# Gated linear attention and top-1 experts on one core: fourth and fifth token chunk routed in one pass, three list steps and four weight casts moved to other engines

## The chip, the cores and the metric

One NeuronCore of a Trainium2 chip runs the whole kernel. Its engines are TensorE (PE in the rows; its weight loads are PEld), VectorE (DVE), ScalarE (ACT), GpSimd (POOL) and the queue engine SyncE (SP). Each engine works through its own instructions in a fixed order, and engines wait for each other by semaphores. The metric is the device time of one execution in microseconds (us); of several executions the median counts.

## What is computed

Two stages, one feeding the other. The first is a linear attention with a decaying state; the second sends every token to one of eight experts. An expert is the argmax of eight logits, except that a token whose local gate is at least 0.5 takes the expert of the token before it, so the choice runs through the sequence.

```python
for t in range(S):                                  # B=4, H=8, S=768, D=48
    state = alpha[:, :, t, :, None] * state + einsum('bhd,bhe->bhde', k[:, :, t], v[:, :, t])
    y[:, :, t] = einsum('bhd,bhde->bhe', q[:, :, t], state)
x = y as (B, S, 384)
for b in range(B):                                  # E=8 experts, F=1024
    for s in range(S):
        e = argmax(logits[b, s]) if s == 0 or local_gate[b, s] < 0.5 else prev_e
        p = softmax(logits[b, s])
        out[b, s] = p[e] * (relu(x[b, s] @ w1[e]) @ w2[e])
```

## The kernel before

The 3072 tokens are 24 **blocks** of 128 tokens: block i is batch i % 4, place i // 4. Four blocks, one of each batch, are a **chunk**; there are six chunks, counted from first to sixth.

**Attention.** The loop `for i in range(NB)` runs over the 24 blocks. `scan1(i + 2)` and `scan2(i + 2)` compute the running products of alpha two blocks ahead: DVE's scans `A` and `sf`, and after each a product on POOL into `ld`. `pm` (PE, PSUM tile `pz`), `mask` (DVE, `pq`), `kt` (`kp`, `kk`), `um` (`up`), `sums` (DVE, `st`), `qm` and `ym` (PE, `py`) make the block's output `XR`, which goes to DRAM (`xd`) and through PE (`xp`, `xx`) into the logits (`lg`, `lt`, `L`).

**Routing.** `route(g)` is a generator that runs for one group of chunks; `SPANS` sets the groups: first and second chunk together, then each of the four others alone. Between its yields the loop resumes it at marked places ("d" for DVE, "p" for PE, "g" for POOL), so that its work lies between that of the blocks. Its steps: the least negated logit `mx`, the comparisons `ge`, the two factors `kr` of the recurrence (DVE); their transposition `rp` (PE); copies `km` (ACT); the scan `em` along the sequence (DVE); back by `rb` (PE) to the one-hot experts `oh`; the counts `oi`, the probability (`ex`, `se`, `pn`, `facts`); the places `pw` (PE), `ps`, and `po`, `where` (DVE). Then each chunk's tokens are put into lists: `spots(a)` takes a place apart into high and low part (`zz`, `hi`, `lo` on POOL), makes the one-hot of the high part `hp` on DVE and its products with the facts on POOL, and the one-hot rows of the low part `lh` on ACT (`low`, five instructions); `lq` (PE) multiplies them, ACT copies the result, POOL adds it to `lists`.

**Early expert.** The first expert's tokens of the first twelve blocks (job `a`) are gathered (`xg_a`) and computed while attention still runs; its later tokens (job `b`) come from the last routing by `fast` (one-hot `hot`, PE `lp`, indices `ix_b`, gather `xg_b`, `tp_b`). Its weights come through three buffers `rw_a`; `Weights.split` makes a high part on ACT (`w1h`, `w2h`) and a remainder (`w1l`, `w2l`). The three pieces of w1 are cast on POOL in halves from the queue `pieces`, one half beside each scan; the four pieces of w2 are cast on DVE. A load into a buffer waits for the cast that frees it. PE's units `h_a` and `yp_a` of job `a` lie between the last blocks and the last routings.

**The rest.** When job `b` is done, seven more experts (`h_r`, `yp_r`) run one after the other.

The program order is kept on every engine (`pinned`, line 97 is the helper that records every operation); nothing is rescheduled.

```python
for w in (slice(0, F // 2), slice(F // 2, F)):
    halves.append(lambda w=w: cast(w, g_, 0.5))
...
for j in range(G):
    s_.activation(lh[:, j], rows[:, 0:128], AF.Abs, bias=lo[:, j:j + 1])
s_.activation(lh, lh, AF.Relu, bias=one[:, 0:1], scale=-1.0)
...
EW.split(SPLITS.index(i), pieces if i <= SPLITS[2] else None)
```

Of the kernel before, what the change touches and what calls it, by code (L numbers as in the profile page):

```python
# [36 lines left out]
G = B  # L37
SPANS = ((0, 2), (2, 3), (3, 4), (4, 5), (5, 6))
T1 = 12
# [33 lines left out]
def gla_moe(ctx, tc, akq, vw, vn, wg, w1, w2, cst, tok, out):  # L73
# [51 lines left out]
    fill = cp.tile([128, 3], F32, name="fill")  # L125
    where = cp.tile([128, NB], F32, name="where")
    facts = cp.tile([128, NB, 3], F32, name="facts")
# [22 lines left out]
    class Weights:  # L150
# [29 lines left out]
        def split(self, p, halves=None):  # L180
# [121 lines left out]
    with ac:  # L302
# [235 lines left out]
        def logits(c, lc):  # L538
            g, j, n = span[c * G]
            lt = pp.tile([128, G, 32], F32, tag="xp", name=f"lt_{c}")  # L540
            t_.transpose(lt.rearrange("p b e -> p (b e)"), lc, ident)
            if j == 0:
                grp[g] = ap.tile([128, n, E + 1], F32, tag=f"L{n}", bufs=1 + (n == G), name=f"L_{g}")
            s_.mul(grp[g][:, j:j + G], lt[:, :, 0:E + 1], -1.0)
            if j + G == n:
                steps.append([route(g), "d"])
            yield

        def route(g):
# [5 lines left out]
            def rt(shape, nm, dt=F32):  # L555
                return ap.tile(shape, dt, tag=f"{nm}{n}", bufs=1 + (n == G and nm in ("pl", "ix", "ps", "em")), name=f"{nm}_{g}")

            L = grp.pop(g)
            L8 = L[:, :, 0:8]
            kr = ap.tile([128, 2, G * max(y - x for x, y in SPANS), 8], F32, tag="kr", bufs=1, name=f"kr_{g}")[:, :, 0:n]  # L560
            ex = rt([128, n, 8], "ex")
# [21 lines left out]
            k0 = km[:, 0]  # L583
            if cb < NBB:
                s_.copy(km, rp)
            else:
                s_.copy(km[:, 1], rp[:, 1])
                k0 = rp[:, 0]
# [40 lines left out]
            xf = where[:, G * ca:G * cb]  # L629
            po = rt([128, n, 8], "po")  # L630
# [8 lines left out]
            while busy[0]:  # L639
                yield "p"  # L640
            high, low, parts = spots(ca)
            for a in range(ca, cb):
                yield "d"
                while not parts:
                    yield "d"
                high()
                yield "p"
                low()
                yield "h" if cb == NBB else "p"
                while len(parts) < 2:  # L650
                    yield "p"
                lq = pp.tile([128, 3 * E * 4], F32, tag="xp", name=f"lq_{a}")
                for j in range(G):
                    t_.matmul(lq, lhsT=lh[:, j], rhs=hp[:, j].rearrange("p c k -> p (c k)"), start=(j == 0), stop=(j == G - 1))
                la = lists.rearrange("p c k -> p (c k)")
                ln = hp[:, 0].rearrange("p c k -> p (c k)") if a else la
                s_.copy(ln, lq)
# [80 lines left out]
        def col(shape, nm, dt=F32):  # L738
            return ap.tile(shape, dt, bufs=1, name=nm)
# [121 lines left out]
        for i in range(NB):  # L861
# [71 lines left out]
        while any(r[1] != "h" for r in steps):  # L933
# [274 lines left out]
```

## Time and profile before

| what | value |
|---|---|
| median of 3 runs | 416.35 us (416.0 to 417.12) |
| the profiled execution itself | 415.97 us |
| its span in the trace | 414.0 us |
| PE busy | 386.2 us (93%) |
| DVE busy | 248.4 us (60%) |
| ACT busy | 182.1 us (44%) |
| POOL busy | 162.6 us (39%) |

The span is the traced stretch from the first to the last instruction; the time of the execution holds some 2 us more around it. The busy shares are means over stages that differ: attention, the last routings beside job `a`, job `b`, and the seven experts. A name in a row, as `po<-ps,oh`, is the tile written and the tiles read.

### The profile page before, as it was taken

The page shows a single profiled execution, that of the slowest core. Times are in us where ns is not written, and L with a number is a line of the kernel's source. Part 1 is how long each engine was busy: PE and PEld are TensorE (multiplying, and loading weights), DVE is VectorE, ACT ScalarE, POOL GpSimd, SP SyncE. Part 2 cuts the span into 40 slices and gives each one's busy share as a digit, 9 for nine tenths or more (in the row PEclk, how much of TensorE's full clock was granted, in tenths as well). Part 3 has the DMA queues.
Part 4 walks back from the last instruction along what each step waited for, and adds up shares of the span by engine and source line. Part 5 has one row for each costly group of instructions (what it writes and reads, how often), then busy time and mean ns, then how long its engine had stood idle before and what let it go on. Part 6 is the DMA issues. An engine that isn't in the chain of part 4 may idle for free.

```text
span 414.0 us, 11455 instructions
## 1 busy us (share of the span) xinstructions
PE 386.2 (93%) x4563; PEld 355.9 (86%) x4563; DVE 248.4 (60%) x569; ACT 182.1 (44%) x450; POOL 162.6 (39%) x232
## 2 busy tenths in 40 slices
PE   7899998989899979999999999999999999999990
PEld 7798877778787869998899999999899899999990
DVE  8879989999887443474572554454364364564310
ACT  2267766678746540362541451352252352453200
POOL 7448666666574010543511432341241241512010
PEclk9889999999999995899999999999999999999996
DMA  8959898887724000564463264175076075461010
GB/s 227 236 161 238 234 296 211 247 229 189 213 62 142 33 8 0 184 194 153 133 180 118 74 198 150 32 234 166 20 220 181 21 222 177 141 185 55 1 40 7
DMA packets 25849, 60.15 MB, mean 145 GB/s; under 512 B 4836, under 2 KB 11318, under 8 KB 25794
## 3 DMA queue, kind: packets, MB, share of 16 engines
q1 hardware_dynamic: 22066, 49.22, 42.2%
q0 software_dynamic: 3584, 10.04, 7.1%
q8 instruction: 36, 0.59, 0.6%
q14 instruction: 19, 0.16, 0.1%
q10 hardware_dynamic: 144, 0.14, 0.1%
HBM read 49.95 MB, written 10.04 MB: 145 GB/s over the span
## 4 chain that ended last, share of the span: by engine, by line
PE 59%; DVE 18%; issue 12%; DMA 4%; POOL 3%; ACT 2%; SPq 0%; DVEq 0%; POOLq 0%; ACTq 0%
PE yp_r L97 19%; PE h_r L97 18%; DVE sf L97 6%; DVE A L97 4%; PE pz L97 3%; DMA ld<-akq 3%; PE yp_a L97 3%; PE py L97 3%; PE yp_b L97 2%; PE h_b L97 2%; PE h_a L97 2%; PE tp_r L97 2%; DVE pq L97 2%; PE up L97 1%; POOL out L97 1%
## 5 line engine op out<-in xcount | busy, mean ns | idle before, releaser
L97 POOL DMA_INDIRECT out<-yo_r,ix_r x25 | 24.7, 987 | 125.2 <-DVE yo_r L97 98.6
L97 PE MATMUL yp_r<-w2h_r,hh_r 128*128 128x384 f32 (+4 forms) x200 | 68.9, 345 | 0.0
L97 PE MATMUL yp_r<-w2h_r,hl_r 128*128 128x384 f32 (+4 forms) x200 | 67.3, 337 | 0.0
L97 PE MATMUL yp_r<-w2l_r,hh_r 128*128 128x384 f32 (+4 forms) x200 | 67.2, 336 | 0.0
L97 PE MATMUL h_r<-xh_r,w1h_r 128*128 128x384 f32 (+5 forms) x168 | 59.9, 356 | 1.0 <-DVE yo_b L97 0.8
L97 PE MATMUL h_r<-xl_r,w1h_r 128*128 128x384 f32 (+5 forms) x168 | 59.6, 355 | 0.0
L97 PE MATMUL h_r<-xh_r,w1l_r 128*128 128x384 f32 (+5 forms) x168 | 59.6, 355 | 0.0
L97 ACT ACTIVATE hh_r<-h_r 128x384 fp32r<-128x384 f32 (+5 forms) x56 | 29.4, 525 | 68.4 <-PE h_r L97 68.2
L97 DVE SCALAR_TENSOR_TENSOR hl_r<-h_r,hh_r 128x384 fp32r<-128x384 f32 (+5 forms) x56 | 33.3, 597 | 33.9 <-ACT hh_r L97 33.6
L97 DVE TENSOR_TENSOR_SCAN sf<-ld,sf,zp 112x128 f32<-112x128 f32 x96 | 38.3, 462 | 0.9
L97 PEld LDWEIGHTS yp_r<-w2l_r,hh_r 128*128 128x128 f32 (+4 forms) x200 | 36.1, 181 | 1.1
L97 PEld LDWEIGHTS yp_r<-w2h_r,hl_r 128*128 128x128 f32 (+4 forms) x200 | 36.0, 180 | 1.2
L97 PEld LDWEIGHTS yp_r<-w2h_r,hh_r 128*128 128x128 f32 (+4 forms) x200 | 36.1, 180 | 1.1
L97 POOL DMA_INDIRECT xg_r<-xd,ix_r x25 | 27.6, 1104 | 19.9 <-PE h_r L97 8.5
L97 ACT CAST xh_r<-tp_r 128x384 fp32r<-128x384 f32 (+4 forms) x25 | 11.4, 455 | 54.2 <-PE tp_r L97 54.2
L97 POOL TENSOR_TENSOR ld<-ld,A 112x512 f32<-112x512 f32 x24 | 28.4, 1182 | 16.5 <-DVE A L97 11.7
L97 PEld LDWEIGHTS h_r<-xh_r,w1h_r 128*128 128x128 f32 x168 | 31.6, 188 | 3.6 <-issue 1.1
L97 POOL TENSOR_TENSOR ld<-ld,sf 112x512 f32<-112x512 f32 x24 | 28.4, 1184 | 14.5 <-DVE sf L97 14.5
L97 PEld LDWEIGHTS h_r<-xh_r,w1l_r 128*128 128x128 f32 x168 | 31.5, 188 | 2.0
L97 PEld LDWEIGHTS h_r<-xl_r,w1h_r 128*128 128x128 f32 x168 | 31.5, 188 | 1.8
L97 DVE TENSOR_SCALAR yo_r<-yp_r,pr 128x384 f32<-128x384 f32 (+4 forms) x25 | 15.4, 616 | 29.4 <-PE yp_r L97 29.4
L97 DVE TENSOR_TENSOR_SCAN A<-ld,zp 112x260 f32<-112x260 f32 x48 | 30.8, 683 | 2.5
(205 smaller groups left out, 795.1 us busy)
## 6 DMA issues: line engine op xcount, KB each, us to landing
rw_r<-w SPq DMA_DIRECT2D x21, 512.0 KB, 4.4
rw_r<-w SPq DMA_DIRECT2D x28, 384.0 KB, 3.6
ld<-akq SPq DMA_DIRECT2D x44, 192.0 KB, 4.4
vt<-vn SPq DMA_DIRECT2D x24, 192.0 KB, 3.5
xd<-XR SPq DMA_DIRECT2D x24, 192.0 KB, 4.1
ld<-akq SPq DMA_DIRECT2D x44, 97.7 KB, 4.5
rw_a<-w SPq DMA_DIRECT2D x3, 512.0 KB, 5.1
rw_a<-w SPq DMA_DIRECT2D x4, 384.0 KB, 4.2
```

The source lines that it names most:

```text
L97: r = f(*a, **k)
```

## The change

The third and fourth group of `SPANS` become one of two chunks, so that the fourth chunk is routed with the fifth, after attention's last block. In `route`, the subtraction `ex` moves ahead of the comparison and serves it (one comparison with zero and multiplication in one instruction), the two transpositions `rp` become one, and the reductions `pn` and `where` become one over `both`. After attention (`drained`), the lists are made by `at_once`: `zz`, `hi`, `lo`, `hp` and `lh` all on DVE, in buffers of their own. The four pieces of the early expert's w2 are cast by POOL, each in one instruction.

```diff
-SPANS = ((0, 2), (2, 3), (3, 4), (4, 5), (5, 6))
+SPANS = ((0, 2), (2, 3), (3, 5), (5, 6))
...
-                for w in (slice(0, F // 2), slice(F // 2, F)):
-                    halves.append(lambda w=w: cast(w, g_, 0.5))
+                for w in (slice(0, F // 2), slice(F // 2, F)) if n < 3 else (slice(None),):
+                    halves.append(lambda w=w: cast(w, g_, 0.5 if n < 3 else 1))
...
+            v_.tensor_tensor(ex, L8, mb, ALU.subtract)
             ge = rt([128, n, 8], "ge")
-            v_.tensor_tensor(ge, L8, mb, ALU.is_le)
-            v_.tensor_tensor(ge, ge, cc("desc").unsqueeze(1).broadcast_to([128, n, 8]), ALU.mult)
+            v_.scalar_tensor_tensor(ge, ex, 0.0, cc("desc").unsqueeze(1).broadcast_to([128, n, 8]), ALU.is_le, ALU.mult)
...
-            for j in range(2):
-                for c in range(m):
-                    t_.transpose(rp[:, j, c * 128:(c + 1) * 128],
-                                 kr[:, j, G * c:G * (c + 1)].rearrange("p b e -> p (b e)"), ident)
+            for c in range(m):
+                t_.transpose(rp[:, c * 128:(c + 1) * 128], kr[:, c].rearrange("p j b e -> p (j b e)"), ident)
...
-            v_.tensor_tensor(ex, L8, mb, ALU.subtract)
...
-            v_.tensor_tensor(ex, ex, ob, ALU.mult)
-            pn = rt([128, n], "pn")
-            v_.tensor_reduce(pn, ex, AX.X, ALU.add)
-            v_.tensor_tensor(facts[:, G * ca:G * cb, 0], pn, se, ALU.mult)
+            po = rt([128, 2, n, 8], "po")
+            v_.tensor_tensor(po[:, 0], ex, ob, ALU.mult)
...
-            v_.tensor_tensor(po, ps[:, :, 0:n].rearrange("p e b -> p b e"), ob, ALU.mult)
-            v_.tensor_reduce(xf, po, AX.X, ALU.add)
+            v_.tensor_tensor(po[:, 1], ps[:, :, 0:n].rearrange("p e b -> p b e"), ob, ALU.mult)
+            v_.tensor_reduce(both[:, :, G * ca:G * cb], po, AX.X, ALU.add)
+            v_.tensor_tensor(facts[:, G * ca:G * cb, 0], both[:, 0, G * ca:G * cb], se, ALU.mult)
...
             for a in range(ca, cb):
+                if drained[0]:
+                    if cb == NBB:
+                        yield "d"
+                    rr = at_once(a)
+                    yield "h" if cb == NBB else "p"
+                    if a == ca and m > 1:
+                        yield "p"
+                    product(a, *rr)()
+                    continue
...
+        def at_once(a):
+
+            lh = ap.tile([128, 2, HP, C], F32, tag="pq", bufs=2, name=f"lh_{a}").rearrange(
+                "p e h t -> p (e h t)").rearrange("p (j t) -> p j t", j=G)
+            hp = ap.tile([128, DM], F32, tag="XR", bufs=3, name=f"hp_{a}").rearrange("p (j c k) -> p j c k", j=G, c=3)
+            x = where[:, G * a:G * (a + 1)]
+            f = facts[:, G * a:G * (a + 1)]
+            z, hi, lo = (ap.tile([128, G], F32, tag=t, bufs=1, name=f"{t}_{a}") for t in ("zz", "hi", "lo"))
+            v_.tensor_scalar(z, x, 1.0 / 128, MAGIC, ALU.mult, ALU.add)
+            v_.tensor_scalar(hi, z, MAGIC + BASE / 128, 128.0, ALU.subtract, ALU.mult)
+            v_.tensor_tensor(hp[:, :, 0], hv.unsqueeze(1).broadcast_to([128, G, E * 4]),
+                             hi.unsqueeze(2).broadcast_to([128, G, E * 4]), ALU.is_equal)
+            for c in (2, 1, 0):
+                g_.tensor_tensor(hp[:, :, c], hp[:, :, 0], f[:, :, c:c + 1].broadcast_to([128, G, E * 4]), ALU.mult)
+            v_.tensor_tensor(lo, x, hi, ALU.subtract)
+            for j in range(G):
+                v_.tensor_scalar(lh[:, j], rows[:, 0:128], lo[:, j:j + 1], None, ALU.is_equal)
+            return lh, hp
...
-                EW.split(SPLITS.index(i), pieces if i <= SPLITS[2] else None)
+                EW.split(SPLITS.index(i), pieces)
...
         drained[0] = True
+        while pieces:
+            pieces.pop(0)()
...
-        EW.split(6)
+        EW.split(6, pieces)
+        while pieces:
+            pieces.pop(0)()
```

How the order moves, at three places. First DVE in the last iteration that scans, between the mask `pq` of block 21 and the end of the scans of block 23. Before:

```order
L97 TENSOR_TENSOR pq_2676<-pz,cs 128x512
L97 SCALAR_TENSOR_TENSOR oi_2678<-m_111,oh_109 128x40
L97 TENSOR_REDUCE se_2680<-ex_2426 128x4
L97 TENSOR_SCALAR se_2680<-se_2680 128x4
L97 RECIPROCAL se_2680<-se_2680 128x4
L97 TENSOR_TENSOR ex_2426<-ex_2426,oh_109 128x32
L97 TENSOR_REDUCE pn_2685<-ex_2426 128x4
L97 TENSOR_TENSOR facts<-pn_2685,se_2680 128x4
L97 TENSOR_TENSOR w2l_a_2647<-rw_a_1881,w2h_a_2646 128x768
L97 MEMSET ld_116 112x4
```

and in the change:

```order
L97 TENSOR_TENSOR pq_2645<-pz,cs 128x512
L97 MEMSET ld_116 112x4
L97 SCALAR_TENSOR_TENSOR A_2679<-ld_116,zp 112x260 x2
L97 RECIPROCAL sf_2685<-A_2679 112x4
L97 SCALAR_TENSOR_TENSOR sf_2685<-ld_116,sf_2685,zp 112x128 x4
L97 TENSOR_TENSOR st_2344<-up_2670,st_2344 112x192
```

The fourth chunk's seven instructions and a cast have left DVE here; nothing stands between mask and scan. Its other instructions have left the two iterations before and the one after in the same way.

Second DVE after the transposed gathers of job `a` (`xl_a`), at the routing that follows the mask of block 23. Before, the fifth chunk alone (32 elements a row):

```order
L97 TENSOR_TENSOR pq_2927<-pz,cs 128x512
L97 TENSOR_TENSOR hp<-hv,hi_2811 128x4x32
L97 TENSOR_REDUCE mx_2932<-L_2849 128x4
L97 TENSOR_TENSOR ge_2934<-L_2849,mx_2932 128x32
L97 TENSOR_TENSOR ge_2934<-ge_2934,cs 128x32
L97 TENSOR_REDUCE m_3_2937<-ge_2934 128x4
```

and in the change, fourth and fifth together (64 elements a row):

```order
L97 TENSOR_TENSOR pq_2870<-pz,cs 128x512
L97 TENSOR_REDUCE mx_2874<-L_2342 128x8
L97 TENSOR_TENSOR ex_2873<-L_2342,mx_2874 128x64
L97 SCALAR_TENSOR_TENSOR ge_2877<-ex_2873,cs 128x64
L97 TENSOR_REDUCE m_2_2879<-ge_2877 128x8
```

The chain has as many instructions as before, and the fourth chunk's `hp` no longer stands ahead of it.

Third POOL, from the last product of attention to the gathers of job `b`. Before:

```order
L97 TENSOR_TENSOR ld_116<-ld_116,sf_2733 112x512
L97 TENSOR_SCALAR zz_2810<-where 128x4
L97 TENSOR_SCALAR hi_2811<-zz_2810 128x4
L97 TENSOR_TENSOR lo_2812<-hi_2811,where 128x4
L97 TENSOR_TENSOR hp<-hp,facts 128x4x32 x3
L97 TENSOR_TENSOR lists<-hp,lists 128x96
```

and in the change:

```order
L97 TENSOR_TENSOR ld_116<-ld_116,sf_2685 112x512
L97 TENSOR_TENSOR w2l_a_2616<-rw_a_1877,w2h_a_2615 128x768
L97 TENSOR_TENSOR w2l_a_2728<-rw_a_2264,w2h_a_2727 128x768
L97 TENSOR_TENSOR w2l_a_2841<-rw_a_2618,w2h_a_2840 128x768
L97 TENSOR_TENSOR w2l_a_3030<-rw_a_2843,w2h_a_3029 128x768
L97 TENSOR_TENSOR hp_3089<-hp_3089,facts 128x4x32 x3
L97 TENSOR_TENSOR lists<-hp_3089,lists 128x96
```

POOL's small place arithmetic is gone, and four casts stand ahead of the fourth chunk's products.

## Rows read from the trace of the kernel before

**Rows 1.** Page, part 2: busy tenths and TensorE's clock in 40 slices.

```profile
DVE  8879989999887443474572554454364364564310
PEclk9889999999999995899999999999999999999996
```

**Rows 2.** Chain that ended last: start us, us, engine, tile written, instructions.

```profile
130.28 1.33 PE h_a L97 x9
...
145.33 0.86 PE pw L97 x6
...
174.83 8.31 PE h_b L97 x72
...
193.68 17.04 PE h_r L97 x72
```

**Rows 3.** Timeline, DVE: start us, us, operation, out<-in, count; routing in attention.

```profile
76.30 0.22 DVE L97 TENSOR_REDUCE pn<-ex 128x8 f32<-128x64 f32 x1
...
108.54 0.18 DVE L97 TENSOR_REDUCE mx<-L 128x4 f32<-128x32 f32 x1
...
110.12 0.06 DVE L97 MEMSET ld<- 112x4 f32 x1 [0.19 <-issue]
...
114.31 0.57 DVE L97 TENSOR_TENSOR_SCAN em<-km,em 32x128 f32<-32x128 f32 x1
...
114.92 0.06 DVE L97 MEMSET ld<- 112x4 f32 x1
...
120.74 0.23 DVE L97 TENSOR_TENSOR_SCAN oi<-m,oh 128x40 f32<-128x40 f32 x1
...
122.15 0.95 DVE L97 TENSOR_TENSOR w2l_a<-rw_a,w2h_a 128x768 fp32r<-128x768 f32 x1
123.05 0.06 DVE L97 MEMSET ld<- 112x4 f32 x1
```

**Rows 4.** Timeline, PE: `qm` of blocks 20 and 21; in brackets, idle before and releaser.

```profile
120.28 0.68 PE L97 MATMUL py<-st,ld 48*64 48x48 f32 x30 [0.60 <-DVE st L97]
...
126.59 0.68 PE L97 MATMUL py<-st,ld 48*64 48x48 f32 x30 [0.44 <-DVE st L97]
```

**Rows 5.** Timeline, PE: the last routings.

```profile
134.82 0.38 PE L97 MATMUL rp<-cs,kr 128*32 128x128 f32 x2 [0.30 <-DVE kr L97]
...
138.03 1.13 PE L97 MATMUL lq<-hp,lh 128*128 128x96 f32 x8
139.54 0.55 PE L97 MATMUL xp<-cs,XR 128*128 128x128 f32 x3 [0.39 <-ACT hp L97]
...
154.03 1.89 PE L97 MATMUL lq<-hp,lh 128*128 128x96 f32 x8 [1.89 <-DVE ex L97]
156.31 0.31 PE L97 MATMUL rb<-cs,em 32*128 32x32 f32 x1 [0.38 <-ACT hp L97]
```

**Rows 6.** Timelines of POOL, DVE and ACT: instructions side by side, and casts.

```profile
123.21 1.27 POOL L97 TENSOR_TENSOR w1l_a<-rw_a,w1h_a 128x512 fp32r<-128x512 f32 x1 [0.37 <-DVE ld L97]
...
126.37 1.19 POOL L97 TENSOR_TENSOR ld<-ld,sf 112x512 f32<-112x512 f32 x1 [0.60 <-DVE sf L97]
...
127.05 0.58 DVE L97 TENSOR_TENSOR po<-ps,oh 128x32 f32<-128x32 f32 x1
...
131.93 0.83 ACT L97 CAST w2h_a<-rw_a 128x768 fp32r<-128x768 f32 x1
...
132.91 0.28 DVE L97 TENSOR_TENSOR hp<-hv,hi 128x128 f32<-128x128 f32 x1
...
146.45 0.22 DVE L97 TENSOR_TENSOR po<-ps,oh 128x32 f32<-128x32 f32 x1 [0.69 <-ACT ps L97]
```

**Rows 7.** PE's first longer wait; then two stretches: PE busy (x), PEld, DVE, ACT, POOL, PEclk, DMA.

```profile
16.50 0.67 PE L97 MATMUL py<-st,ld 48*64 48x48 f32 x16 [1.26 <-DVE st L97]
...
17.70:24.20 6.50, 6.50 (x92) 5.87 (x91) 4.15 (x11) 2.03 (x8) 2.35 (x2) 0.50 0.68 154
154.20:167.60 13.40, 13.02 (x51) 12.71 (x51) 4.67 (x27) 0.72 (x4) 2.52 (x4) 0.50 0.05 13
```

More of the change, by code (lines that the diff above doesn't have):

```diff
@@ L125, in gla_moe @@
     fill = cp.tile([128, 3], F32, name="fill")
-    where = cp.tile([128, NB], F32, name="where")
+    both = cp.tile([128, 2, NB], F32, name="both")
+    where = both[:, 1]
     facts = cp.tile([128, NB, 3], F32, name="facts")
@@ L555, in rt @@
             def rt(shape, nm, dt=F32):
-                return ap.tile(shape, dt, tag=f"{nm}{n}", bufs=1 + (n == G and nm in ("pl", "ix", "ps", "em")), name=f"{nm}_{g}")
+                return ap.tile(shape, dt, tag=f"{nm}{n}", bufs=1, name=f"{nm}_{g}")
             L = grp.pop(g)
             L8 = L[:, :, 0:8]
-            kr = ap.tile([128, 2, G * max(y - x for x, y in SPANS), 8], F32, tag="kr", bufs=1, name=f"kr_{g}")[:, :, 0:n]
+            kr = ap.tile([128, max(y - x for x, y in SPANS), 2, G, 8], F32, tag="kr", bufs=1, name=f"kr_{g}")[:, 0:m]
             ex = rt([128, n, 8], "ex")
@@ L572, in route @@
             v_.tensor_tensor(ge, ge, m2.unsqueeze(2).broadcast_to([128, n, 8]), ALU.is_equal)
-            zb = L[:, :, 8:9].broadcast_to([128, n, 8])
-            v_.scalar_tensor_tensor(kr[:, 0], zb, -ZTHR, ge, ALU.is_gt, ALU.mult)
-            v_.tensor_single_scalar(kr[:, 1], zb, -ZTHR, ALU.is_le)
+            zb = L[:, :, 8:9].rearrange("p (c b) e -> p c b e", b=G).broadcast_to([128, m, G, 8])
+            v_.scalar_tensor_tensor(kr[:, :, 0], zb, -ZTHR, ge.rearrange("p (c b) e -> p c b e", b=G), ALU.is_gt, ALU.mult)
+            v_.tensor_single_scalar(kr[:, :, 1], zb, -ZTHR, ALU.is_le)
             yield "p"
-            rp = pp.tile([8 * G, 2, m * 128], F32, tag="xp", name=f"rp_{g}")
-            for j in range(2):
-                for c in range(m):
-                    t_.transpose(rp[:, j, c * 128:(c + 1) * 128],
-                                 kr[:, j, G * c:G * (c + 1)].rearrange("p b e -> p (b e)"), ident)
+            rp = pp.tile([16 * G, m * 128], F32, tag="xp", name=f"rp_{g}")
+            for c in range(m):
+                t_.transpose(rp[:, c * 128:(c + 1) * 128], kr[:, c].rearrange("p j b e -> p (j b e)"), ident)
             km = ap.tile([8 * G, 2, 128 * max(y - x for x, y in SPANS)], F32, tag="km", bufs=1, name=f"km_{g}")[:, :, 0:m * 128]
-            k0 = km[:, 0]
+            s_.copy(km[:, 1], rp[8 * G:])
+            k0 = rp[0:8 * G]
             if cb < NBB:
[L585 to L588, printed above, removed]
+                s_.copy(km[:, 0], k0)
+                k0 = km[:, 0]
             yield "d"
@@ L640, in route @@
                 yield "p"
-            high, low, parts = spots(ca)
+            if not drained[0]:
+                high, low, parts = spots(ca)
             for a in range(ca, cb):
+                if drained[0]:
[7 more added lines that the diff above has]
+                    continue
                 yield "d"
@@ L648, in route @@
                 low()
-                yield "h" if cb == NBB else "p"
+                yield "p"
                 while len(parts) < 2:
                     yield "p"
[L652 to L657, printed above, removed]
+                add = product(a, lh, hp)
                 busy[0] = False
@@ L661, in route @@
                 yield "g"
-                if a:
-                    g_.tensor_tensor(la, ln, la, ALU.add)
-                listed.append(a)
+                add()
             if cb * G == T1:
@@ L669, in route, with product, add @@
                 gathers.append(0)
+        def product(a, lh, hp):
+            lq = pp.tile([128, 3 * E * 4], F32, tag="xp", name=f"lq_{a}")
+            for j in range(G):
+                t_.matmul(lq, lhsT=lh[:, j], rhs=hp[:, j].rearrange("p c k -> p (c k)"), start=(j == 0), stop=(j == G - 1))
+            la = lists.rearrange("p c k -> p (c k)")
+            ln = hp[:, 0].rearrange("p c k -> p (c k)") if a else la
+            s_.copy(ln, lq)
+            def add():
+                if a:
+                    g_.tensor_tensor(la, ln, la, ALU.add)
+                listed.append(a)
+            return add
+        def at_once(a):
[12 more added lines that the diff above has]
+            v_.tensor_tensor(lo, x, hi, ALU.subtract)
+            for j in range(G):
+                v_.tensor_scalar(lh[:, j], rows[:, 0:128], lo[:, j:j + 1], None, ALU.is_equal)
+            return lh, hp
         def spots(a):
@@ L937, in gla_moe @@
             n += 1
-        both = col([128, 2, E], "both")
+        rest = col([128, 2, E], "rest")
         pick3 = big
         v_.tensor_tensor(pick3, hot8.rearrange("p r e -> p e r"), caps.unsqueeze(1).broadcast_to([128, E, E]), ALU.mult)
-        v_.tensor_reduce(both[:, 0], pick3, AX.X, ALU.add)
-        v_.tensor_tensor(both[:, 1], cF, both[:, 0], ALU.subtract)
+        v_.tensor_reduce(rest[:, 0], pick3, AX.X, ALU.add)
+        v_.tensor_tensor(rest[:, 1], cF, rest[:, 0], ALU.subtract)
         jobs = [jb]
@@ L965, in gla_moe @@
         ct = pp.tile([8, 2, 128], F32, tag="kp", name="ct")
-        t_.transpose(ct[:, 0], both[:, 0], ident)
-        t_.transpose(ct[:, 1], both[:, 1], ident)
+        t_.transpose(ct[:, 0], rest[:, 0], ident)
+        t_.transpose(ct[:, 1], rest[:, 1], ident)
         v_.tensor_copy(capp, ct[:, 0, 0:1])
```

3 lines of the change are left out of this document (1 added, 2 removed).

## The prediction, made before the changed kernel ran

> **What bounds the kernel now.** I read the busy tenths first, then the chain of waits, then the timelines engine by engine around what the change moves. Each of the 40 slices is 10.35 us long. DVE stands at 8 or 9 tenths up to the 13th slice, and the clock row shows one slice near half speed, the 16th [rows 1]. So attention, up to about 126 us, goes at DVE's pace, and an instruction that leaves DVE there can shorten it. The chain then changes over to PE: from the first `h_a` at 130.28 us it runs through PE's work, job b starts at 174.83 and the first of the seven experts at 193.68 [rows 2]. The edits end before `h_b`, and what follows is the same code with its own loads behind the same gather. A shift at `h_b` is therefore a shift of the end. I work out that shift; minus means earlier. The profiled execution took 415.97 us, 0.38 under the median of 416.35; sums stand against it, and 0.4 is added for forecasts.
>
> **Attention: fewer instructions on DVE.** The first two groups each lose two small instructions. A reduction of 64 elements takes 0.22 us, one of 32 takes 0.18 [rows 3], and the joint reduction is longer by that difference or two of them; I take -0.3 for a group, -0.6 for both, between 0 (if a wait swallows it) and -0.9.
>
> The fourth chunk leaves three iterations at DVE's pace: from `mx` to the next memset 110.12 - 108.54 = 1.58, from `em` 114.92 - 114.31 = 0.61, from `oi` 123.05 - 120.74 = 2.31 us, the last with a cast from 122.15 to 123.05 [rows 3]. The first two count in full. In the third, PE becomes the slower one. PE's `qm` waited for DVE's `st` at 120.28 and again at 126.59, the second time 0.44 us [rows 4]. Between the two lie 6.31 us; without that wait and without a `pw`, 0.86 [rows 2], PE needs 5.0, while DVE would need 6.31 - 2.31 = 4.0. So this iteration gives 6.31 - 5.0 = 1.3. Together -(0.6 + 1.58 + 0.61 + 1.3) = **-4.1** at `h_a`, between -5.1 (DVE alone) and -3.1 (one of ACT's or the loads' steps takes back 1 us). The transpositions and copies that are merged or split ride under DVE here and count nothing; should PE or ACT be last somewhere, that is the 1 us.
>
> Queues: POOL's gathers `xg_a` stand ahead of the casts and are not delayed. On SP, the load of the last early weight piece moves behind one store, since its buffer now comes free only after POOL's first cast. What covers that: its cast on ACT stands behind the last block's `ym`, two units of `h_a` later. Nothing on DVE or PE asks for a `w2l` before `yp_a`, after `rb`.
>
> **After attention: a wait that the casts bring.** At 126.37 POOL began a product of 1.19 us, to 127.56; DVE's `po` beside it took 0.58 us from 127.05, to 127.63, where the same instruction with POOL idle took 0.22 [rows 6]. So a DVE instruction that reads two tiles of SBUF is held until POOL's instruction ends. POOL casts half a piece, 512 columns, in 1.27 us [rows 6]; a w2 piece has 768, so 1.27 x 768/512 = 1.9. Before, DVE made these casts.
>
> The third cast waits for ACT's `w2h`, which in the rows ended at 131.93 + 0.83 = 132.76; both it and DVE's mask hang on the first `h_a`, so they keep their distance. POOL starts at about 132.86. DVE's chain for `kr` now starts where `hp` stood, 132.91 [rows 6]. Its pace is 1.58/7 = 0.23 per instruction at 32 elements [rows 3], 0.26 at 64. Its second instruction, the first with two inputs in SBUF, wants to start at 133.17, finds POOL busy and is held to 134.76. Six instructions of 0.26 later, 136.3, `rp` can go. PE is there at 134.82 - 0.30 = 134.52 [rows 5]: it waits 1.8 us instead of 0.30, **+1.5**. The bounds are -0.1 (no hold: the chain ends at 134.73) and +1.9 (held for a whole cast). I take +1.5, because `po` was held to the end of POOL's instruction and not merely slowed. If the two only slowed each other as much as that row shows, 0.58 - 0.22 = 0.36, the chain would end near 135.1 and the sum below would be 1.2 less.
>
> The Trainium skill's page "SBUF — State Buffer" (section "Who interferes with whom") has a rule that speaks against this change: a VectorE instruction with two SBUF inputs and a GpSimd instruction that reads SBUF share one read interface, and whichever starts first keeps it for its whole instruction. By that rule the hold is a whole cast's; the trace agrees as far as it goes, since `po` ended 0.07 us after POOL [rows 6], but it shows no hold as long as 1.9 us.
>
> **After attention: what goes and what comes.** The fourth chunk's `lq` leaves its place: 139.54 - 138.03, **-1.5** [rows 5]. It comes back beside the fifth's. Before, from the last `h_a` to `rb`: `lq` at 154.03 had waited 1.89 for ACT's `lh`, so that `h_a`, 1.33 long [rows 2], began at 150.8, and 5.5 us passed to 156.31 [rows 5]. Now two `lq` with their copies, 1.5 each, one `h_a` of 1.3, and a short wait for POOL's products, taken as 0.4 (estimate: the list's addition and three products beside one `h_a`), make 4.7: **-0.8**, between -1.9 (the old wait goes whole) and 0. `lh` and `hp` on DVE count nothing: before the first `lq` they lie under two `h_a`, 2.6 us; without that cover they would cost their length, some 2 us.
>
> **The clock.** PE had 1.2 GHz in two stretches: 17.7 to 24.2, soon after a wait of 1.26 us, and 154.2 to 167.6, after the wait of 1.89 [rows 5, 7]. In the second, `yp_a`, `pw` and `lp` ran. In the change the wait of 1.89 goes, but short `lq`, waits and small matmuls follow each other there, so I leave the clock in the last routing as it was: 0. The bounds: 0, and half of the 11.3 us from `rb` to 167.6, -5.7, if it stays at 2.4 GHz.
>
> **Sum:** -4.1 + 1.5 - 1.5 - 0.8 = -4.9; 415.97 - 4.9 = 411.1, on the median **411.4 us**.
>
> **Rivals.**
>
> No hold at `rp`: -4.9 - 1.6 = -6.5, 409.9. For it: 0.3 us of order decides who comes first. Against: the cast lasts longer than the whole chain.
>
> The clock stays at 2.4 GHz through the last routing: PE would gain up to 5.7 but then wait for DVE's indices and the gather of job b, which a faster PE doesn't shorten; between 0 and 5.7 I take -3.5: -8.4, 408.0. For it: the long wait is gone. Against: the dense work there is not denser.
>
> The clock falls at the new wait before `rp`. It lies between the two waits after which it fell [rows 5, 7]. For the shorter stretch seen, 6.5 us, half is lost, 3.2: -1.7, 414.7; some of it covers other waits, so 413.5 to 415. Against: dense `h_a` stands on either side, and waits of 0.4 to 0.6 us never did it [rows 4]. The Trainium skill's page "TensorE: Matmul & The Clock Gate" (section "Why this matters for your kernels") blames only idle gaps longer than any in this stage; by that rule this rival falls away and the forecast gets its chance. The trace disagrees: both falls followed shorter gaps [rows 5, 7].
>
> Slower: the same fall lasting as long as the second stretch, 13.4 us, because the clock came back only in a long run of `yp_a`. It costs half, 6.7: +1.8, 418.2. It decides from a stretch of 9.8 us on, twice the gain. Against: `h_a` is denser than `lp`.
>
> DVE's pace in attention is taken over by PE, ACT or loads at once: half of the 4.1, 413.5. Against: DVE's 9 tenths [rows 1]. That the change doesn't do what it says I leave out: the order shows the instructions gone.
>
> **How the numbers follow.** Forecast 0.40; no hold 0.12; clock stays 0.12; clock falls at `rp`, short, 0.27; long 0.05; attention half 0.04. The range is 407.4 to 415.2: from the clock that stays to the short fall, with the bounds of attention (1 us either way) inside; it leaves out the long fall and the tails. About 0.3%, 1.25 us, is what a measurement of this kernel can tell from no change. Slower by more is the long fall, 0.05; within it lie the top of the short fall and bits of others, 0.08; faster is the rest, 0.87.
>
> **What would show it.** Right: `h_a` begins near 126.2; no DVE routing beside the scans of blocks 21 to 23; DVE's `ex` for 64 elements taking over 1 us beside a POOL `w2l_a`; PE waiting 1.5 to 2 us before `rp`; `rb` near 151.4; `h_b` near 170. Wrong: `h_a` later than 127.5 (attention is not DVE's alone); `ex` at 0.25 us (no hold); the clock at 1.2 GHz between 132 and 145, or at 2.4 GHz from `rb` to `h_b`.

## The result and the profile after

The changed kernel took 409.39 us (median of 4 runs, 408.82 to 411.39) against 416.18 us before (median of 4, 415.37 to 417.12): ratio 0.9845, 95% interval 0.9805 to 0.9885. The ratios here leave out executions more than 1.5% above the fastest of their kernel; medians and ranges hold all. The profiled execution took 409.14 us, its span is 407.3, so `h_b` and all behind it came 6.6 us earlier. From the two traces, stage by stage:

| stretch | before | after | difference | forecast |
|---|---|---|---|---|
| start to first `h_a` | 130.28 | 127.87 | -2.41 | -4.1 |
| first `h_a` to `rp` | 4.54 | 5.69 | +1.15 | +1.5 |
| `rp` to third `h_a` | 5.03 | 3.54 | -1.49 | -1.5 |
| third `h_a` to last `rb` | 16.46 | 16.21 | -0.25 | -0.8 |
| last `rb` to `h_b` | 18.52 | 14.88 | -3.64 | 0 |
| sum | | | -6.64 | -4.9 |

The total was met; the terms for attention and for the clock were not. The busy tenths and the clock on the changed kernel's page (40 slices) answer to [rows 1]:

```profile
DVE  8789988999884476575562472563453454564310
...
PEclk9999999999999999999999999999999999999996
```

The slow 16th slice is gone. The chain that ended last, of the changed kernel (start us, us, engine, tile), answers to [rows 2]:

```profile
127.87 1.29 PE h_a L97 x9
...
142.65 0.89 PE pw L97 x6
...
168.19 8.31 PE h_b L97 x72
...
187.00 17.04 PE h_r L97 x72
```

DVE's timeline (start us, us, operation, out<-in) of the kernel before, the scans that open the last iterations, and then of the changed kernel:

```profile
103.48 1.28 DVE L97 TENSOR_TENSOR_SCAN A<-ld,zp 112x260 f32<-112x260 f32 x2
...
110.22 1.28 DVE L97 TENSOR_TENSOR_SCAN A<-ld,zp 112x260 f32<-112x260 f32 x2
...
115.03 1.28 DVE L97 TENSOR_TENSOR_SCAN A<-ld,zp 112x260 f32<-112x260 f32 x2
...
123.16 1.28 DVE L97 TENSOR_TENSOR_SCAN A<-ld,zp 112x260 f32<-112x260 f32 x2
```

```profile
103.73 1.28 DVE L97 TENSOR_TENSOR_SCAN A<-ld,zp 112x260 f32<-112x260 f32 x2
...
108.92 1.28 DVE L97 TENSOR_TENSOR_SCAN A<-ld,zp 112x260 f32<-112x260 f32 x2
...
113.23 1.28 DVE L97 TENSOR_TENSOR_SCAN A<-ld,zp 112x260 f32<-112x260 f32 x2
...
119.16 1.28 DVE L97 TENSOR_TENSOR_SCAN A<-ld,zp 112x260 f32<-112x260 f32 x2
...
130.71 1.57 DVE L97 TENSOR_TENSOR ex<-L,mx 128x64 f32<-128x64 f32 x1
```

From scan to scan the changed kernel takes 5.19, 4.31 and 5.93 us instead of 6.74, 4.81 and 8.13: DVE gained 1.55, 0.50 and 2.20. But from the last scan to the first `h_a` it takes 8.71 instead of 7.12, so 1.6 of that goes back. The last row is the held subtraction `ex`; POOL's cast beside it, from POOL's timeline:

```profile
130.38 1.81 POOL L97 TENSOR_TENSOR w2l_a<-rw_a,w2h_a 128x768 fp32r<-128x768 f32 x1 [2.20 <-ACT w2h_a L97]
```

PE's timeline of the changed kernel (in brackets, idle before and its releaser), answering to [rows 4, 5]:

```profile
121.38 0.56 PE L97 MATMUL py<-vt,pq 64*64 64x48 f32 x12 [0.40 <-issue]
...
133.56 0.38 PE L97 MATMUL rp<-cs,kr 128*64 128x128 f32 x2 [1.49 <-DVE kr L97]
...
149.46 0.30 PE L97 MATMUL rp<-cs,kr 128*64 128x128 f32 x1 [0.37 <-ACT hp L97]
...
151.74 1.10 PE L97 MATMUL lq<-hp,lh 128*128 128x96 f32 x8 [0.92 <-DVE em L97]
153.31 0.24 PE L97 MATMUL rb<-cs,em 32*128 32x32 f32 x1 [0.46 <-ACT hp L97]
```

The wait of 1.89 before `lq` is down to 0.92, that before `rp` up from 0.30 to 1.49. Last, the second stretch of [rows 7] in the changed kernel (PE, PEld, DVE, ACT, POOL busy; then PEclk):

```profile
154.20:167.60 13.40, 11.81 (x81) 11.14 (x79) 8.55 (x40) 1.09 (x3) 4.33 (x6) 1.00 0.35 102
```

It ran at 2.4 GHz, not at 1.2.

### The profile page after: what moved, and what is told of

Its sections match the earlier page's. It is cut to its first block, busy times and chain, and to the rows that moved or that the text cites. A ratio compares the mean times of both kernels' runs of the same rounds, so it can differ in the third digit from the quotient of the medians.

```text
span 407.3 us, 11412 instructions
## 1 busy us (share of the span) xinstructions
PE 378.1 (93%) x4551; PEld 348.1 (85%) x4551; DVE 246.5 (61%) x560; ACT 176.2 (43%) x434; POOL 167.2 (41%) x227
## 4 chain that ended last, share of the span: by engine, by line
PE 71%; issue 12%; DVE 10%; POOL 2%; ACT 2%; DMA 1%; SPq 0%; POOLq 0%; DVEq 0%; ACTq 0%
PE yp_r L97 20%; PE h_r L97 19%; PE py L97 7%; PE pz L97 5%; PE up L97 3%; DVE sf L97 3%; PE yp_b L97 2%; PE h_b L97 2%; PE h_a L97 2%; DVE A L97 2%; PE tp_r L97 2%; PE lq L97 1%; POOL out L97 1%; PE kp L97 1%; PE lg L97 1%
```

## The experiments

**Theory** after the comparison: half of the gain is the clock, and it stays up because DVE's one-hot rows take away PE's wait of 1.89 us; the joint routing shortens attention; the third cast on POOL costs 1.2. **Rivals:** the clock falls or not by chance, whatever the change; DVE is still the bound and needs the casts on POOL; the joint routing brings nothing. In the expectations "fourth and fifth group" are those chunks. All runs were timed in several executions; the mean clock is PE's over one execution (1 is 2.4 GHz):

| kernel | median us | range | mean clock | ratio to before, 95% |
|---|---|---|---|---|
| before, three sets | 415.04, 415.92, 415.48 | 411.06 to 423.08 | 0.952 to 0.988 | |
| changed, again (e6) | 409.82 | 405.71 to 414.34 | 0.964 to 0.989 | 0.9827 (0.9765 to 0.9889) |
| e1, last two casts on DVE | 407.36 | 406.75 to 408.21 | 0.977 to 0.985 | 0.9823 (0.9780 to 0.9867) |
| e2, rows by ACT | 415.00 | 412.56 to 419.65 | 0.945 to 0.973 | 1.0027 (0.9986 to 1.0068) |
| e3, routed apart | 408.58 | 406.13 to 410.37 | 0.976 to 0.984 | 0.9863 (0.9815 to 0.9911) |
| e4, before + rows by DVE | 409.18 | 406.61 to 410.71 | 0.983 to 0.992 | 0.9857 (0.9808 to 0.9907) |
| e5, before + filled wait | 412.14 | 407.73 to 414.19 | 0.977 to 0.990 | 0.9946 (0.9911 to 0.9982) |
| e7, e1 + own bank | 409.11 | 402.74 to 411.94 | 0.962 to 0.988 | 0.9757 (0.9659 to 0.9856) |
| e8, all casts on DVE | 406.07 | 405.50 to 407.38 | 0.979 to 0.988 | 0.9775 (0.9729 to 0.9821) |
| e9, e8 + early fill | 406.89 | 403.99 to 412.04 | 0.960 to 0.990 | 0.9779 (0.9717 to 0.9841) |
| e10, e9 + late fills | 407.64 | 402.74 to 412.55 | 0.974 to 0.993 | 0.9761 (0.9693 to 0.9830) |
| e11, e10 + own bank | 406.25 | 404.73 to 407.76 | 0.979 to 0.993 | 0.9797 (0.9748 to 0.9845) |
| e12, e8, routed apart | 408.16 | 405.18 to 409.79 | 0.972 to 0.989 | 0.9848 (0.9792 to 0.9904) |

The times scatter with the clock, so the traces are compared by stretches as well. From DVE's scan `A` that begins between 100 and 105 to the first matmul of `h_b` in PE's timeline pass 71.1 us in the kernel before, 64.2 in the changed kernel (66.7 in e6, where the clock fell), 64.1 in e4, 63.6 in e3 and in e12, 62.9 in e1, 62.2 in e8 and 61.4 in e7. In the timeline `h_b` begins 0.2 us ahead of its piece of the chain above.

### The rows and the clock: e2, e4, e5, e6

e2, in the changed kernel's `at_once`:

```diff
-            v_.tensor_tensor(lo, x, hi, ALU.subtract)
+            v_.tensor_tensor(lo, hi, x, ALU.subtract)
             for j in range(G):
-                v_.tensor_scalar(lh[:, j], rows[:, 0:128], lo[:, j:j + 1], None, ALU.is_equal)
+                s_.activation(lh[:, j], rows[:, 0:128], AF.Abs, bias=lo[:, j:j + 1])
+            s_.activation(lh, lh, AF.Relu, bias=one[:, 0:1], scale=-1.0)
```

> The changed kernel with the one-hot rows of the last groups made by ACT in five instructions again instead of four by DVE; all else as changed. Theory (the wait before the last `lq` is what drops the clock, and DVE's rows took it away): PE waits 1.9 us or more before an `lq` between 148 and 155, the clock is at 1.2 GHz afterwards for 3 to 14 us, `h_b` starts 2.5 to 6 us later, time 412 to 415. Rival (the clock falls or not by chance, whatever the rows are made by): the wait is longer by up to 1 us, mean clocks of the runs scatter as those of the changed kernel (0.970 to 0.988), time 409.5 to 410.5.

PE's timeline of e2, and two stretches of its trace at 1.2 GHz:

```profile
134.25 0.38 PE L97 MATMUL rp<-cs,kr 128*64 128x128 f32 x2 [1.49 <-DVE kr L97]
...
155.57 1.99 PE L97 MATMUL lq<-hp,lh 128*128 128x96 f32 x8 [2.56 <-DVE em L97]
157.94 0.31 PE L97 MATMUL rb<-cs,em 32*128 32x32 f32 x1 [0.37 <-ACT hp L97]
```

```profile
134.60:138.00 3.40, 3.40 (x40) 3.31 (x40) 0.83 (x2) 1.20 (x3) 0.00 (x0) 0.50 0.03 12
155.10:172.30 17.20, 16.36 (x62) 15.99 (x63) 7.13 (x35) 2.95 (x10) 4.24 (x7) 0.50 0.08 24
```

One edit undone, and the gain is gone: 415.00. `lq` waits 2.56, the clock falls at 155.1 for some 17 us. The mean clock is under 0.970 in 11 of e2's 12 executions and in 1 of the 10 of the changed kernel. It also fell behind the wait of 1.49 before `rp`: the forecast's rival of a short fall there is real, if not in every execution.

e4 is the reverse: the kernel before, with `at_once` and `product` for the fifth and sixth chunk alone.

```diff
+                if ca >= 4:
+                    if cb == NBB:
+                        yield "d"
+                    rr = at_once(a)
+                    yield "h" if cb == NBB else "p"
+                    product(a, *rr)()
+                    continue
```

> The kernel before with one part of the change alone: the one-hot rows of the fifth and sixth group by DVE in one go. Theory: the wait of 1.89 us before the fifth group's `lq` falls to under 1, `rb` comes 0.5 to 1.5 earlier, the clock stays at 2.4 GHz from `rb` to `h_b`, which saves 3.6 more; attention is as before (first `h_a` near 130.3): time 411 to 412.5. Rival (the clock falls there by chance): `rb` 0.5 to 1.5 earlier, the clock falls as before in most runs, time 414.7 to 415.7, mean clock about 0.967.

It is as fast as the whole change, 409.18. `lq` waits for nothing. It goes ahead of `rp` on PE now, and ACT's rows are gone; PE's timeline of e4, then ACT's, then ACT's and DVE's of the kernel before:

```profile
150.96 1.03 PE L97 MATMUL lq<-hp,lh 128*128 128x96 f32 x8
152.91 0.38 PE L97 MATMUL rp<-cs,kr 128*32 128x128 f32 x2
154.38 0.24 PE L97 MATMUL rb<-cs,em 32*128 32x32 f32 x1
```

```profile
153.39 0.25 ACT L97 COPY km<-rp 32x128 f32<-32x128 f32 x1
```

```profile
151.22 1.27 ACT L97 ACTIVATE lh<-rows,lo 128x128 f32<-128x128 f32 x4
152.52 0.72 ACT L97 ACTIVATE lh<-lh,one 128x512 f32<-128x512 f32 x1
153.15 0.24 ACT L97 COPY km<-rp 32x128 f32<-32x128 f32 x1
```

```profile
153.42 0.47 DVE L97 TENSOR_TENSOR_SCAN em<-km,em,rp 32x128 f32<-32x128 f32 x1 [1.64 <-ACT km L97]
```

Before, `km` stood on ACT behind 2 us of rows, `em` on DVE behind `km`, and `lq` behind `em`, which reads `rp` in the bank that `lq` was to take. Now `rb` comes 22.9 us behind the first `h_a` instead of 26.0: 3.2 earlier, over twice what I expected. From `rb` to `h_b` e4 takes 14.5 us at 2.4 GHz. e4 moves the rows and the order of `lq` and `rp` at once, so it doesn't part the two; e2 moves the rows alone. Its gain is also made up otherwise than that of the change: e4 has no gain in attention (26.8 us from that scan to `h_a`), while the change gains 2.7 there and has `rb` 25.4 us behind `h_a`, not 22.9. So the other edits of the change together brought nothing beyond e4: what they gain in attention they lose between `h_a` and `rb`.

e5 parts the wait from the work: the kernel before, its wait filled, nothing else moved.

```diff
+                if a == 4:
+                    fz = pp.tile([128, ja.n], F32, tag="up", name="fz")
+                    for _ in range(15):
+                        t_.matmul(fz, lhsT=EW.w1[0][0][:, 0:128], rhs=ja.xh[:, 0, :], start=True, stop=True)
                 lq = pp.tile([128, 3 * E * 4], F32, tag="xp", name=f"lq_{a}")
```

> The kernel before with 15 matmuls of the size of `h_a`'s into a free bank between the last `h_a` and the fifth group's `lq`: they take some 1.8 us of PE's wait of 1.89 and change nothing else. Theory (the idle wait lets the clock fall, and the fall is what the one-hot rows by DVE saved beside the wait itself): `lq` and `rb` start as far behind the first `h_a` as before (23.7 and 26.0 us), the clock stays at 2.4 GHz from `rb` to `h_b` in most runs, mean clocks 0.98 and over, median 411 to 412. Rival (the clock falls for what comes behind, the small matmuls of the last routing): the clock falls as before, median 414.5 to 416, mean clocks 0.967 to 0.984 as for the kernel before.

```profile
149.09 1.86 PE L97 MATMUL fz<-xh_a,w1h_a 128*128 128x256 f32 x15
151.15 1.10 PE L97 MATMUL lq<-hp,lh 128*128 128x96 f32 x8 [0.20 <-DVE ex L97]
152.63 0.24 PE L97 MATMUL rb<-cs,em 32*128 32x32 f32 x1 [0.38 <-ACT hp L97]
```

```profile
152.60:167.00 14.40, 12.92 (x88) 12.34 (x88) 7.86 (x36) 3.29 (x10) 5.57 (x10) 1.00 0.34 102
```

Those are PE's timeline and the stretch from `rb` to `h_b`. `lq` starts 23.8 us behind the first `h_a`, as before; it takes 1.10 instead of 1.89 because the clock is up, and it stays up. (This execution had no fall near 16 us either: its first `h_a` comes at 127.39, 2.9 earlier than in the kernel before, whose instructions up to there are the same. Its own 407.73 us thus says little of the fill; the twelve executions do.) All 12 executions have mean clocks of 0.977 and over, while 9 of the 17 of the kernel before beside them have less than 0.970. Useless work in a wait made the kernel faster: 3.8 us by the medians, 0.9946 by the ratio. Over these executions the wait is shown to be what let the clock fall for the long stretch from `rb` on; the rival that the small matmuls behind it do that alone falls. A short fall of 3.4 us right behind `lp` still comes without such a wait in e3, e10 and e12.

e6 is the changed kernel once more.

> The changed kernel as it is, beside the others on their chip, for the scatter of its clock and time. If its clock stays up by the change: all runs within 2 us above the fastest, mean clocks 0.975 and over, median 408.5 to 409.5. If that was chance: some runs with mean clocks under 0.97 and times over 412.

PE's `lq` and a stretch of its trace:

```profile
151.16 1.10 PE L97 MATMUL lq<-hp,lh 128*128 128x96 f32 x8 [0.92 <-DVE em L97]
```

```profile
153.50:163.80 10.30, 10.30 (x43) 10.30 (x42) 4.83 (x29) 0.17 (x1) 2.06 (x3) 0.50 0.07 19
```

So chance has a part: behind the wait of 0.92 the clock fell in this execution, and from `rb` to `h_b` took 3.2 us longer than in the first trace. By the mean clocks the change makes the fall rarer (under 0.970 in 1 of its 10 executions, in 18 of 45 of the kernel before), and where a trace shows it, it lasted 10 us (e6) instead of 13; the change doesn't end it. And the trace that comes with a result is one draw.

### The casts: e1, e8

```diff
-                EW.split(SPLITS.index(i), pieces)
+                EW.split(SPLITS.index(i), pieces if i < SPLITS[5] else None)
...
-        EW.split(6, pieces)
-        while pieces:
-            pieces.pop(0)()
+        EW.split(6)
```

> The changed kernel with the last two of the four w2 casts back on DVE. Theory (the third cast holds DVE's `ex`, which took 1.57 us beside it): `ex` takes 0.2 to 0.3 us, PE waits at most 0.3 us before `rp` instead of 1.49, `rp` starts 1.2 us earlier against the first `h_a`, and the time falls by 1.2, to about 408.2. Rival (the earlier `rp` is only waited for again, at `pw` for ACT or at the last `lq`): `rp` earlier by 1.2, `h_b` by under 0.4, time 409 to 409.4. Rival (the chain for `kr` is late for another reason than the cast): the wait before `rp` stays over 1 us, time 409.4.

DVE's timeline of e1, then PE's:

```profile
131.34 0.22 DVE L97 TENSOR_TENSOR ex<-L,mx 128x64 f32<-128x64 f32 x1
```

```profile
132.86 0.38 PE L97 MATMUL rp<-cs,kr 128*64 128x128 f32 x2
```

`ex` took 0.22 instead of 1.57, PE waited for nothing, `rp` came 4.39 us behind the first `h_a` instead of 5.69: the cast is shown as the cause, at 1.3 us. `rb` kept it (24.1 behind `h_a` instead of 25.4). The Trainium skill's page "SBUF — State Buffer" (section "SBUF: two separate sides") says that the one that starts first keeps the shared read interface for its whole instruction; the trace agrees, for `ex` ended at 132.28, 0.09 us after POOL's cast.

e8 goes on, with `i <= SPLITS[2]` in that condition.

> The changed kernel with all four w2 casts on DVE, as before the change. Theory (PE sets the last iterations of attention by now and DVE waits 0.9 and 2.7 us there, so that POOL's first two casts free nothing): the first `h_a` as far behind the scan that starts near 104 as in the changed kernel (24.1 us, within 0.3), PE waits at most 0.3 before `rp`, time as with two casts on DVE, 407 to 407.8. Rival (DVE is the bound there still): first `h_a` later by 0.9 to 1.9 us, time 408 to 409.2.

DVE's and PE's timelines of e8:

```profile
118.17 0.95 DVE L97 TENSOR_TENSOR w2l_a<-rw_a,w2h_a 128x768 fp32r<-128x768 f32 x1
...
123.06 1.63 DVE L97 TENSOR_TENSOR w2l_a<-rw_a,w2h_a 128x768 fp32r<-128x768 f32 x1
```

```profile
126.30 0.39 PE L97 MATMUL h_a<-xh_a,w1h_a 128*128 128x256 f32 x1 [0.23 <-DVE xl_a L97]
```

The first `h_a` comes 23.35 us behind the scan at 102.95; in e6, with the casts on POOL, 23.32 behind the scan at 103.94. POOL's casts freed nothing: DVE has the room. (24.1, which I expected, holds 0.8 us of waits of PE that e6 and e8 don't have.) With 406.07 against 415.92 before and 409.82 for the change beside it, this is the lowest median, though e11's 406.25 is as good within the noise; its interval overlaps that of the change. In the traces `rb` of e8 comes 1.3 us earlier behind the first `h_a` than in the change.

### The joint routing: e3, e12, e7

e3 puts the old `SPANS` back in the changed kernel (two buffers for `em` of a single chunk); e12 does so in e8.

```diff
-SPANS = ((0, 2), (2, 3), (3, 5), (5, 6))
+SPANS = ((0, 2), (2, 3), (3, 4), (4, 5), (5, 6))
```

> The changed kernel with the fourth and the fifth group routed apart again; the shorter routing, DVE's late rows and POOL's casts stay. Theory: the first `h_a` starts 2 to 2.5 us later than 127.87 (the fourth group's mask and shares are back in DVE's attention), the `lq` of 1.5 us is back between `rp` and `rb`, the third cast still holds the chain for `kr`, the clock stays at 2.4 GHz at the end of routing: time 412.5 to 413.5. Rival (the joint routing brings nothing, PE's own work sets attention's last iterations): first `h_a` within 0.7 of 127.87, time 410 to 411.

> The changed kernel with all four w2 casts on DVE and the fourth and fifth group routed apart, beside the run with the casts on DVE alone (406.1): what the joint routing is worth by itself. Theory (it frees 2.7 us of attention and gives back 1.3 between the first `h_a` and `rb`, where two `lq` now stand at the end): first `h_a` some 26.5 us behind the scan that begins near 103 instead of 23.35, `rb` 22.9 behind the first `h_a` instead of 24.1, time 407 to 408.5. Rival (the whole of it is given back, as it seemed with POOL's casts): time 405.5 to 406.5.

e3 went against me: 408.58, not 412.5. Its first `h_a`, at 127.98, looks as if routing apart cost nothing, but its clock didn't fall near 16 us and its scan began at 101.90: from there 26.1 us passed, as in e12, against 23.3 to 24.1. DVE's scan and PE's rows of e12:

```profile
102.87 1.28 DVE L97 TENSOR_TENSOR_SCAN A<-ld,zp 112x260 f32<-112x260 f32 x2
```

```profile
128.96 0.39 PE L97 MATMUL h_a<-xh_a,w1h_a 128*128 128x256 f32 x1 [0.23 <-DVE xl_a L97]
...
148.34 1.02 PE L97 MATMUL lq<-hp,lh 128*128 128x96 f32 x8
150.30 0.27 PE L97 MATMUL rp<-cs,kr 128*64 128x128 f32 x1
151.76 0.25 PE L97 MATMUL rb<-cs,em 32*128 32x32 f32 x1
```

So the joint routing does free 2 to 2.7 us of attention. What I had missed comes behind it. POOL's timeline of e3:

```profile
131.04 1.29 POOL L97 TENSOR_TENSOR hp<-hp,facts 128x128 f32<-128x128 f32 x3 [1.74 <-DVE mx L97]
132.28 1.85 POOL L97 TENSOR_TENSOR w2l_a<-rw_a,w2h_a 128x768 fp32r<-128x768 f32 x1
```

Routed apart, the fourth chunk's products stand ahead of the third cast, which then starts too late to hold DVE's `ex` (131.02 to 131.21). And `rb` comes 22.8 us behind the first `h_a`, in e3 as in e12, against 24.1 in e1 and e8: apart, the fifth chunk's `lq` goes ahead of `rp`; joint, the fourth's takes that place, and the fifth's stands behind `em` in the shared bank, with `rb` behind it. Against the same casts (e12 and e8), the joint routing gains 2.7 and returns 1.3; the medians, 408.16 and 406.07 from different sets, have the sign of that, and their intervals overlap.

e7 tests what holds the last `lq`: e1, with its bank changed.

```diff
-            lq = pp.tile([128, 3 * E * 4], F32, tag="xp", name=f"lq_{a}")
+            lq = pp.tile([128, 3 * E * 4], F32, tag="up" if drained[0] and a < NBB - 1 else "xp", name=f"lq_{a}")
```

> The changed kernel with the last two w2 casts on DVE and the fourth and fifth groups' `lq` in the bank that `lg` has left, not in the one that `rp` and `rb` share with it. Theory (in the joint routing the last `lq` waits for `em`, because that reads `rp` from the shared bank, and `rb` waits for the copy of `lq`): `lq` waits only for DVE's rows, up to 0.3 us instead of 0.92, `rb` starts 1 to 1.3 us earlier against the first `h_a` than in the run with two casts on DVE alone (24.1), time 406 to 406.5. Rival (DVE's rows and scan set that stretch, not the bank): `rb` at 23.7 to 24.1 behind the first `h_a`, time 407.0 to 407.5.

PE's timeline of e7:

```profile
148.94 1.13 PE L97 MATMUL lq<-hp,lh 128*128 128x96 f32 x8 [0.94 <-POOL hp L97]
150.01 0.24 PE L97 MATMUL rb<-cs,em 32*128 32x32 f32 x1
```

`rb` is 23.1 behind the first `h_a`, 1.0 earlier, as expected; but `lq` waits as long as before, now for POOL's products, and only `rb` is freed. The time missed: its best execution, 402.74, is with one of e10's the fastest of all, its worst 411.94 at a mean clock of 0.962. Where the clock falls in those isn't seen; the profiled one shows only an early fall.

### Other waits: e9, e10, e11

```diff
+            if i == 1:
+                fx = pp.tile([128, 240], F32, tag="xp", name="fx")
+                for _ in range(10):
+                    t_.matmul(fx, lhsT=dz[:, 0:128], rhs=dz[:, 0:240], start=True, stop=True)
             if i:
                 qm(i - 1)
...
+                busy_pe("z", 7)
...
+        busy_pe("pe", 12)
```

The first part is e9; `busy_pe(tag, n)`, ahead of the fifth chunk's `lq` and of `ct`, issues n matmuls like e5's and is added in e10; e11 adds e7's edit.

> The changed kernel with all four w2 casts on DVE, and 10 matmuls into an unused bank in PE's wait of 1.26 us near 16 us, behind which the clock fell in nine of the ten traces so far. Theory (that wait lets the clock fall, and the fall costs 2 to 3 us in attention, since the scan that begins near 100.6 in the trace without it begins at 102.9 to 104.7 in those with it): no fall before 30 us, that scan near 101, mean clocks 0.985 and over, time 403.5 to 404.5. Rival (DVE sets attention's pace, so an early fall is covered): that scan at 102.5 or later, time 405.5 to 406.5 as without the matmuls.

> The same, with 7 matmuls of `h_a`'s size in PE's wait of 0.92 us before the fifth group's `lq` and 12 in its wait of 1.5 us before `ct` besides. Theory: the late fall, which the changed kernel has still in some runs, goes; all mean clocks 0.985 and over, times within 1.5 us of each other, 403 to 404. Rival (the waits left are too short to matter, or the small matmuls between them make the clock fall): as with the early matmuls alone.

> The same with the late groups' `lq` in a bank of their own. Theory: `rb` 23.1 us behind the first `h_a` instead of 24.1, and with the clock held up the scatter of 402.7 to 411.9 that this edit had is gone: time 402 to 403. Rival (the fall in that version comes from what stands behind `rb`): scatter over 4 us again, median 405 or more.

(The first of these miscounts: the clock fell there in eight of ten traces; e3 and e5 are without.) PE's timeline and one stretch of e9:

```profile
15.33 1.37 PE L97 MATMUL fx<-dz 128*128 128x240 f32 x10
```

```profile
55.60:59.30 3.70, 3.70 (x70) 3.04 (x69) 0.89 (x2) 1.25 (x5) 1.18 (x1) 0.54 0.55 136
```

The fall behind the wait of 1.26 is gone in all three, but another came near 55, within 2 us behind a wait of PE of 1.77, 1.22 and 1.50 that has no releaser in the profile ("issue"); e10 fell again near 88 and near 157. The scan near 104 began at 104.55, 103.87 and 103.63: nothing gained, and the time doesn't beat e8's. e10's and e11's late matmuls themselves waited for a bank, 0.45 and 1.01 us, and pushed `rb` back by 0.4 and 0.9. A fill is no cure where a wait of another kind follows. e11 narrowed the range of e7 to 3 us, at a median of 406.25 instead of the 402 to 403 expected.

## Why the prediction was right, and where it was wrong

The time, 409.39, lies 2 us below the forecast of 411.4 and inside the range. The sum is right for partly wrong reasons, and its closeness is luck in part: attention gave 1.7 us less than forecast and the clock 3.6 more, and the two partly cancel. Two of the signs that the prediction named for being wrong came true: the first `h_a` at 127.87, later than 127.5, and the clock at 2.4 GHz from `rb` to `h_b`.

1. **Attention, -4.1: right in kind, met in part.** The DVE row of [rows 1] reads 7, not 8 or 9, in the 3rd and the 13th slice. The iterations gave what the rows had (1.55 of 1.58, 0.50 of 0.61, 2.20 of 2.31), and PE took over as forecast. The first two groups gave 0.40 of 0.6, from the scan at 71.54 (before 70.89) to that at 103.73. Short was what PE left: 0.6 instead of 1.3. From `qm` to `qm` PE needed 5.98 us in the first trace, not 5.0; e6, the same program, shows 5.14, without the wait of 0.40 at 121.38 and smaller ones beside it. By e6, scan to `h_a` falls from 26.80 to 23.32, 3.48, and the three terms said 1.58 + 0.61 + 1.3 = 3.49. The 0.65 by which the scan near 71 is late, for which no edit stands, makes up the rest; in that place DVE waits 0.52 for PE's `pz` (0.25 in e6, nothing in the kernel before), and why stays open.
2. **The hold, +1.5: right, 1.2 measured.** PE waited 1.49 instead of the 1.8 forecast, and `ex` 1.57; e1 removes it. The rival "no hold" falls. What the forecast left unsaid is that nothing pays for the cast: e8.
3. **The fourth chunk's `lq`, -1.5: right** (1.49). Its return, -0.8, was too good: 0.25. For the wait before the last `lq` I took 0.4 as an estimate from POOL's products; it was 0.92, for `em`, by way of a shared bank, and `rb` waited 0.46 more. In a bank of its own `lq` waited as long for POOL's products (0.94 in e7), so the estimate of these was too short by itself.
4. **The clock, 0: the step that failed.** I wrote that the wait goes but that short `lq`, waits and small matmuls follow, and left the clock as it was. The wait was the cause (e5, by the mean clocks of its executions), and with it shortened to 0.92 the stretch took 3.64 us less, the price of the rival "clock stays" (-3.5), to which I gave 0.12. It should have had the larger part: [rows 5, 7] show the fall within 0.2 us of this wait's end and 1.2 us behind that of the early one, and none in the stages where PE only waited 0.6 [rows 4]. e6 shows that the forecast's own case also occurs. The short fall at `rp` (0.27) occurred in e2's trace, in neither of the changed kernel's.
5. **"`lh` and `hp` on DVE count nothing": wrong.** By their length they are covered, as I said. But where they had stood counted: ACT's rows were in front of `km`. An edit that moves them, with the order of `lq` and `rp`, makes the gain by itself (e4), and without the rows on DVE there is none (e2).

The rule from the Trainium skill's page "TensorE: Matmul & The Clock Gate" (section "Why this matters for your kernels") blames idle gaps longer than any shown here. That idle gaps matter, the runs agree; their length they contradict: filling 1.89 us (e5) and 1.26 us (e9) took the falls behind them away, the first by the mean clocks of twelve executions, the second in three traces of three.

## What to carry to other kernels

Before costing an instruction that moves off an engine, look at what stands behind it there: ACT's rows cost 2 us not by themselves but through the copy, the scan and the bank queued behind them. Where PE's clock falls right behind a wait, count the clock to that wait; a kernel that puts matmuls nobody reads into it tests whether that is so, if it is timed in several executions. And an edit that frees an engine is worth something only as far as the next engine lets it: the casts moved to POOL freed a DVE that already waited.

## What the runs showed of the hardware

- One program, different clocks. The kernel before took 411.06 us at a mean clock of 0.984 and 420.39 at 0.959, on one chip: a spread larger than the change.
- What stood before the falls in the 14 traces, up to 2 us before them: behind 1.89 and 2.56 before `lq` the clock fell in 2 of 2; behind the 1.26 near 16 us in 9 of the 11 that have it; behind waits of 1.05 to 1.77 without a releaser near 54 in 4 of 6, behind 1.24 without one near 66 in none of 2; behind 1.27 near 72 in e2, the one trace that has it; behind 0.87 to 0.89 at an earlier `rp` near 88 in 2 of 11 (e1, e10); behind 1.49 at `rp` in 1 of 3; behind 0.92 to 0.94 at `lq` in 1 of 6; behind 1.45 to 1.71 before `ct` in none of 7. In e3, e10 and e12 it fell near 156 with no wait of note, right behind `lp`'s small matmuls, for 3.4 us; from `rb` to `h_b` that cost e12 0.2 us against e4, since PE waits there anyway (1.50 before `ct` in e4, nothing in e12). What decides in which execution it falls stays open.
- PE's waits without a releaser differ between executions of one program: 0.40 at 121.38 in the first trace of the changed kernel, none there in the second.
- A hold by POOL lasted 1.3 us here, where [rows 6] had shown 0.4.
